# An attention and gMLP block on one core: matrix-engine warm-up matmuls, a last output block in two column halves, and new written-out task orders

## The chip, the cores and the metric

The kernel runs on one core of a Trainium2 chip. The metric is the device time of that core in microseconds (us). The kernel before took 248.39 us (median of 3 runs, 246.49 to 248.95). A core has five engines with a queue of instructions each: PE multiplies matrices (its weight loads have a row of their own, PEld), DVE and ACT work on vectors, POOL does small things, and SP here only issues DMAs. ACT issues a few DMAs too. An engine takes its instructions strictly in the order in which they were written; between engines there are semaphores.

## The reference

The input x is 2048 tokens by 448 features in bf16. Two residual blocks follow each other:

```python
h  = x + A(layernorm(x))          # local attention
h2 = h + B(layernorm(h))          # gMLP
# A: q, k, v = x @ wqkv, 16 heads of 28; token t sees the 8 tokens t, t-2, ..., t-14
#    o = softmax(q k / sqrt(28)) v;  o @ wo
# B: z = gelu(x @ w_in) (1792 columns), z1 = first 896, z2 = layernorm(last 896)
#    g = w_sp @ z2 + b_sp  (2048 x 2048 over the tokens);  (z1 * g) @ w_out
```

## The kernel before

Tokens are held in 16 blocks of 128; block u and block u+8 are worked on together as "unit" u (8 units), on the two halves of the partitions. The work is cut into 667 tasks, each for one engine, with names used here and in the prediction:

- `x0` to `x15`, `xhalo`, `wq`, `wk`, `wv`, `win`, `wsp`: loads (L723, L758, L730, L742, L1124). `wsp` and `tD` are transposing DMAs.
- `bn1`, `rs1`, `nrm1` (L818, L808 or L830, L838): first layer norm of a block: statistics, reciprocal deviation, normalised block. `bnh`, `rsh`, `nrmh`, `tTh`, `evh` do it for the 16 halo rows.
- `tT1_u` with `ev1_u` (L854, L803/L805), or `tD1_u` (L845): unit u transposed by PE and copied out of PSUM, or by a DMA. Units 0 to 2 go the first way.
- `cpq`, `cpk` (L803 on ACT, L805 on DVE): four copies each that spread the loaded q and k weights; the last digit of the name is the column half. `mmq2_0`, `mmk0_2` and so on (L965): q and k projections of a token chunk (first number) for two head groups (or one, in chunk 3); `evq`, `evk` copy them out of PSUM.
- For each attention tile i of nine: `mmv` (L1005, 28 matmuls), `mml` (L1040, 64), `exp` (L1053), `mask` (L1060), `mmr` (L1069), `ln` and `rex`, `mmo` (L1089, 64), `ot` (L1107). Then per unit `mmy` (L1143) and `h` (L1151), and the second layer norm.
- `mmz2` with `ge`, `bn3`, `ag3`, `rs3`, `nrm3` (L1163, L1173, L1179, L1185, L809, L1193): z2 and its layer norm. `mmz1`, `gz1` (L1207, L1217): z1.
- `g` (L1244): the token mixing, 28 groups of 16 matmuls; the first three groups (0_0, 0_1, 0_2) are cut into eight pieces of two, one per unit. `ua`, `um` (L1254, L1262) add the bias and multiply by z1. `wo` (L1273), `oa` (L1281), `st` (L1285): output product, residual and store of each block.

The order of the tasks on every engine is written out: `SEQ` (L41 to L72) holds a list of task numbers per engine, for SP, POOL, DVE, ACT and PE. `Planner.replay` walks the five lists with a model of durations; the model does not change the order, but it picks the PSUM banks and other buffers by the free times it computes. It would also put dummy matmuls (`fill`, L795, on the constant tile `warm`) into predicted idle stretches of PE, provided that the memset of `warm` (`c_warm`) already stands behind it in the walk. In the list of DVE `c_warm` stands among the last tasks, so no dummy matmul is put anywhere. `Sched.issue` turns reads and writes into semaphore waits.

Of the kernel before, what the change touches and what calls it, by code (L numbers as in the profile page):

```python
# [33 lines left out]
PHASES = [(range(0, 9), range(0, 8))]  # L34
WPEN = 200
MPEN = 10.704
OFF = {"q": -124.25, "v": 1265.42, "evv": 569.01, "l": -1263.94, "exp": -259.78, "mask": -1085.83, "r": -1027.56, "o":
       -1264.27, "ln": 1046.18, "ot": 511.44, "y": -65.14, "h": 108.86, "ln2": -195.97, "z2": -1857.43, "ge": 2334.62,
       "n3": 1020.58, "x0": -60.60, "xd": 242.96, "evq": 1087.78, "cp": 975.37, "td": 561.22, "cw": -627.08}
ADJ = ()  # L40
SEQ = (  # L41
# [30 lines left out]
)  # L72
O_AFTER_LN = True
NBANKS = 8
TU = 26.48
NE = 2
NL = 2
NV = 3
SET_E = "natural_log_exp_and_others"
SET_G = "gelu_apprx_tanh_and_others"  # L80

# [152 lines left out]
class Planner:  # L234
# [19 lines left out]
    def pick(self, p, n):  # L254
# [5 lines left out]
        if n == 1:  # L260
            single = sorted((s for s in free if s ^ 1 not in free), key=lambda s: free[s])
            if single:
                return [single[0]]
# [1079 lines left out]
```

## Time and profile before

| | before |
|---|---|
| time, median of 3 runs | 248.39 us (246.49 to 248.95) |
| profiled execution, span | 247.4 us |
| PE busy | 232.1 us, 94% of the span |
| DVE busy | 143.3 us, 58% |
| ACT busy | 91.4 us, 37% |
| POOL busy | 28.8 us, 12% |
| granted clock | 1.00 |

The span runs from the first to the last instruction of the profiled execution, its page gives no other time for it. The span lies inside the three timed runs: 1.0 us under their median and 0.9 us over the fastest. An engine that is not the one everything waits for may idle at no cost; the chain of work that ended last tells which stretches count.

### The profile page before, as it was taken

What the parts mean: (1) busy time and instruction counts of PE and PEld (TensorE: products, weight loads), DVE (VectorE), ACT (ScalarE), POOL (GpSimd) and SP (SyncE); (2) the same over time, 40 slices, a digit from 0 to 9 for tenths busy, and PEclk for the clock granted to TensorE, in tenths of its full rate; (3) what the DMA queues carried; (4) which work ended last, traced back from release to release, by engine and by line L of the source; (5) the groups of instructions that cost most, each with busy time, mean ns of one, the idle gap of its engine ahead of it and who ended that gap; (6) DMA issues with size and microseconds to landing.
All of it is one profiled execution on the core that took longest, in us unless ns stands there. A gap on an engine that the chain in (4) does not pass through costs nothing.

```text
span 247.4 us, 6649 instructions
## 1 busy us (share of the span) xinstructions
PE 232.1 (94%) x3004; PEld 123.7 (50%) x3004; DVE 143.3 (58%) x281; ACT 91.4 (37%) x103; POOL 28.8 (12%) x69
## 2 busy tenths in 40 slices
PE   0399799999999999999999999999999999999995
PEld 0297485445556555555544444444444444444442
DVE  6697847779999897798970022335021407541743
ACT  2668784886979965575740000000000000000000
POOL 2843010000021112104530000000000000000000
DMA  6935965893224976886733333100000000010113
GB/s 159 255 80 61 138 91 98 128 154 71 46 40 85 152 197 124 180 147 150 108 85 85 87 85 85 42 3 0 0 0 0 3 0 0 2 46 29 56 57 111
DMA packets 54436, 20.02 MB, mean 81 GB/s; under 512 B 46584, under 2 KB 54280, under 8 KB 54408
## 3 DMA queue, kind: packets, MB, share of 16 engines
q1 hardware_dynamic: 52584, 18.05, 37.4%
q10 hardware_dynamic: 1824, 1.55, 2.8%
q8 instruction: 23, 0.38, 0.7%
q14 instruction: 5, 0.04, 0.1%
HBM read 6.39 MB, written 1.84 MB: 33 GB/s over the span
## 4 chain that ended last, share of the span: by engine, by line
PE 93%; DMA 3%; issue 1%; ACT 1%; ACTq 1%; DVE 0%
PE psum L1244 39%; PE psum L965 11%; PE psum L1163 9%; PE psum L1273 9%; PE psum L1207 9%; PE psum L1005 5%; PE psum L1143 5%; DMA z2p<-in_A_wqkv_dram 3%; PE psum L1040 3%; PE psum L1089 2%; PE psum L1069 1%; ACT reg L803 1%; ACTq L723 1%; ACT xh L803 0%; ACTq L730 0%
## 5 line engine op out<-in xcount | busy, mean ns | idle before, releaser
L1254 DVE TENSOR_TENSOR ub<-psum,reg 128x512 bf16<-128x512 f32 x28 | 18.8, 687 | 64.3 <-PE psum L1244 64.2
L1244 PE MATMUL psum<-reg,z2p 128*128 128x512 bf16 x224 | 50.0, 379 | 0.0
L1244 PE MATMUL psum<-wspT_lo,z2p 128*128 128x512 bf16 x224 | 49.0, 379 | 0.0
L1244 PEld LDWEIGHTS psum<-wspT_lo,z2p 128*128 128x128 bf16 x224 | 21.8, 98 | 26.6 <-issue 0.4
L1244 PEld LDWEIGHTS psum<-reg,z2p 128*128 128x128 bf16 x224 | 21.9, 98 | 26.1
L965 PE MATMUL psum<-xh,reg 64*128 64x128 bf16 (+3 forms) x448 | 28.5, 290 | 2.8 <-issue 2.0
L965 PEld LDWEIGHTS psum<-xh,reg 64*128 64x128 bf16 x448 | 19.4, 105 | 10.5 <-issue 3.4
L1163 PE MATMUL psum<-w_in,xh 64*128 64x448 bf16 x224 | 22.5, 349 | 0.0
L1273 PE MATMUL psum<-reg 128*128 128x448 bf16 x112 | 22.3, 352 | 0.0
L1207 PE MATMUL psum<-xh,w_in 64*128 64x512 bf16 x196 | 22.2, 376 | 0.0
L818 DVE BATCH_NORM_STATS2 st<-x_tm 128x6 f32<-128x448 bf16 x32 | 19.5, 609 | 1.0 <-DMA x_tm<-in_A_x_dram 0.8
L1179 DVE BATCH_NORM_STATS2 st<-z2p 128x6 f32<-128x448 bf16 x32 | 17.7, 612 | 2.6 <-ACT z2p L1173 2.5
L803 ACT ACTIVATE reg<-psum 128x896 bf16<-128x896 f32 (+3 forms) x21 | 16.8, 824 | 5.8 <-PE psum L965 4.2
L1053 ACT ACTIVATE reg<-psum 128x928 bf16<-128x928 f32 x18 | 16.1, 943 | 6.4 <-PE psum L1040 6.4
L1281 DVE TENSOR_TENSOR tring<-psum,x_tm 128x448 bf16<-128x448 f32 x16 | 9.6, 616 | 14.0 <-PE psum L1273 14.0
L808 POOL TENSOR_SCALAR rs<-mv 128x2 f32<-128x2 f32 x21 | 6.3, 300 | 93.7 <-DVE mv L819 78.4
L1173 ACT ACTIVATE z2p<-psum 128x896 bf16<-128x896 f32 x16 | 14.2, 916 | 6.8 <-PE psum L1163 6.8
L1163 PEld LDWEIGHTS psum<-w_in,xh 64*128 64x128 bf16 x224 | 11.9, 94 | 9.5 <-issue 0.9
L1217 ACT ACTIVATE reg<-psum 128x1024 bf16<-128x1024 f32 x14 | 13.7, 1030 | 7.8 <-PE psum L1207 7.8
L1273 PEld LDWEIGHTS psum<-reg 128*128 128x128 bf16 x112 | 11.0, 98 | 10.6
L1207 PEld LDWEIGHTS psum<-xh,w_in 64*128 64x128 bf16 x196 | 11.1, 94 | 9.7
L809 POOL TENSOR_TENSOR rs<-rs,nhalf 128x2 f32<-128x2 f32 x21 | 15.6, 743 | 1.8
(63 smaller groups left out, 201.2 us busy)
## 6 DMA issues: line engine op xcount, KB each, us to landing
out_dram<-tring SPq DMA_DIRECT2D x16, 112.0 KB, 1.7
x_tm<-in_A_x_dram SPq DMA_DIRECT2D x13, 112.0 KB, 5.7
w_in<-in_B_w_in_dram SPq DMA_DIRECT2D x2, 448.0 KB, 5.5
z2p<-in_A_wqkv_dram ACTq DMA_DIRECT2D x2, 392.0 KB, 6.3
reg<-in_B_w_out_dram SPq DMA_DIRECT2D x1, 784.0 KB, 4.8
w_in<-in_B_w_in_dram SPq DMA_DIRECT2D x2, 336.0 KB, 5.1
reg<-in_B_b_sp_dram SPq DMA_DIRECT2D x1, 512.0 KB, 4.2
reg<-in_A_wo_dram SPq DMA_DIRECT2D x4, 98.0 KB
```

Source lines behind the costliest of these rows:

```text
L803: iss("act", lambda e: e.activation(dst, src, AF.Copy), reads=rd, writes=wr)
L809: iss("pool", lambda e: e.tensor_tensor(dst, dst, nh, ALU.pow), reads=rr + [r_nhalf], writes=rr)
L818: iss("dve", lambda e: e.bn_stats(st[:, b, :], x_tm[:, b, :]), reads=[r_x[b]], writes=[rl[b]])
L965: iss("pe", lambda e, c=c, s=s, gi=gi, lhs=lhs: e.matmul(psum[:, bk[s] * 512 + cw * gi:bk[s] * 512 + cw * gi + cw], lhs, xh[64 * s:64 * s ...
L1053: iss("act", lambda e: e.activation(E[:, es[0], 2 * n:2 * n + 2, :], pair_view(lb, 0, 8 * JW), AF.Exp, scale=SCALE), reads=[r_bank[lb[0]], ...
L1163: iss("pe", lambda e, c=c, s=s: e.matmul(psum[:, zb[s] * 512:zb[s] * 512 + D], xh[64 * s:64 * s + 64, c, HX + 128 * u:HX + 128 * u + 128], ...
L1173: iss("act", lambda e: e.activation(z2p[:, u:u + 9:8, D * k:D * k + D], pair_view(zb, 0, D), AF.Gelu_apprx_tanh), reads=[r_bank[zb[0]], r_ ...
L1179: iss("dve", lambda e, b=b: e.bn_stats(st3[:, b, k, :], z2p[:, b, D * k:D * k + D]), reads=[r_z2[b][k]], writes=[r_st3[b][k]])
L1207: iss("pe", lambda e, c=c, s=s: e.matmul(psum[:, bk[s] * 512:bk[s] * 512 + 512], w_in[64 * s:64 * s + 64, c, 128 * f:128 * f + 128], xh[64 ...
L1244: iss("pe", lambda e, b=b: e.matmul(psum[:, gb[0] * 512:gb[0] * 512 + 512], z2p[:, b, 128 * f:128 * f + 128], src[:, b, 512 * (tc % 2):512 ...
L1254: iss("dve", lambda e: e.tensor_tensor(ub[:, us_[0], :], psum[:, gb[0] * 512:gb[0] * 512 + 512], bb[:, 512 * tc:512 * tc + 512], ALU.add), ...
L1273: iss("pe", lambda e, f=f: e.matmul(psum[:, wb[0] * 512:wb[0] * 512 + D], z1p[f][:, 128 * m:128 * m + 128], w_out[:, f, :], start=(f == 0) ...
```

## The change

1. `c_warm` comes second on DVE instead of near the end. Three new PE tasks hold dummy matmuls of 512 columns on `warm`: `f0` (15, the first task of PE), `f1` (3, after `tT1_0`) and `f2` (3, after `tT1_1`). They write a PSUM bank that nobody reads. The old way of placing fillers is gone.
2. Block 15, the last to be stored, is computed in two halves of 224 columns: its 7 matmuls of 448 columns become 14 of 224, its `oa` and its store become two each. A half has its own PSUM bank and its own slot of the store ring.
3. The constants of the planner's model are different, which can change bank numbers only, and the heuristic scheduler that was unused is deleted.
4. All five lists are new. The heads of the lists, by name (`mml0` and `mmo0` stand for the four tasks of a tile, in the last line `mml3+mml2` for eight that alternate):

```text
SP    before  x0 xhalo x4 x3 x10 x7 x6 x2 x5 x11 wo2 x12 x13 x15 tD1_3 x14 wo3 win1_0 tD1_4 tD1_7 tD1_6 tD1_5
      after   xhalo x0 x4 x3 x5 x11 x13 x7 x2 x10 x12 x6 wo1 x15 tD1_3 x14 win1_0 tD1_5 tD1_7 tD1_6 tD1_4
POOL  before  c_wkp c_wqp c_nhalf c_ident c_eps rs1_1 rsh c_mband c_V c_xpad c_kpad rs1_2
      after   c_V c_eps c_nhalf c_ident c_wkp rsh c_wqp c_kpad c_xpad rs1_3 c_mband c_ones
DVE   before  c_th0 c_wo0 bn1_0 bn1_1 bn1_8 bn1_9 nrm1_0 bnh nrm1_8 nrm1_1 nrm1_9 cpq10 nrmh cpk01 cpk10
              cpq11 evh bn1_2 bn1_10 cpk11 bn1_11 bn1_12 nrm1_2 bn1_3 nrm1_10 bn1_4 cpv10 nrm1_3 nrm1_11
      after   c_th0 c_warm c_wo0 bnh bn1_9 bn1_0 bn1_1 bn1_8 nrm1_1 nrm1_9 nrm1_0 nrmh nrm1_8 cpk11 ev1_0
              cpk00 cpk10 evh cpq01 bn1_11 bn1_3 cpq00 bn1_10 nrm1_3 bn1_2 nrm1_11 cpv10 bn1_13 nrm1_2
ACT   before  x1 x8 x9 wk wq c_tab rs1_0 cpk00 cpq00 ev1_1 ev1_0 evq1_0 wv evk1_0 cpq01 evq0_0 evk1_2 evk0_0
      after   x9 x1 x8 wk wq c_tab rs1_1 rs1_0 cpk01 ev1_1 cpq11 wv cpq10 evk1_2 evk0_0 evk1_0 evq0_2 evq0_0 evk0_2
PE    before  tT1_0 tT1_1 tTh mmq1_0 mmk1_0 mmq0_0 mmk0_0 mmk1_2 mmq0_2 mmk0_2 mmq1_2 tT1_2 mml0 mmv1 mmv0
              mml1 mmv2 mmq2_0 mmr0 mmr1 mmq2_2 mmk2_2 mmk2_0 mmo0 mmv3 mmo1 mml2 mmq3_1
      after   f0 tT1_1 f2 tT1_0 f1 tTh mmk1_2 mmk1_0 mmk0_0 mmk0_2 mmq0_2 mmq0_0 mmq1_2 mmq1_0 mml0 mmv1 mmv0
              tT1_2 mml1 mmr0 mmq2_2 mmk2_2 mmq2_0 mmk2_0 mmo0 mmr1 mmv2 mmv3 mmo1 mml3+mml2 mmq3_2
```

Further on, the last `mmz2` of PE (`mmz2_6_1`) is followed by eight `mmz1` tasks instead of six, and the token mixing starts with `g0_2_0 g0_6_0 g0_1_0 g1_3_0` instead of `g0_2_0 g0_2_1 g0_2_2 g0_1_0 g0_1_1 g0_0_0 g0_0_1 g0_1_2 g0_6_0`. From `g0_4_0` on the order of PE is the same as before up to its end, which is now `wo12_6 wo14_6`, then for block 15 the first six matmuls of either half and the seventh of either half.

The core of the diff, without the lists and the deleted scheduler:

```diff
+        def fill(name, n, deps=()):
+            fb = []
+
+            def em():
+                for _ in range(n):
+                    iss("pe", lambda e: e.matmul(psum[:, fb[0] * 512:fb[0] * 512 + 512], warm[:, 0:128], warm[:, :]),
+                        reads=[r_warm], writes=[r_bank[fb[0]]])
+            return add(name, "pe", 0.216 * n, em, deps=[c_warm] + list(deps), acq=[("ps", 1, fb)], rel=[("ps", fb)], mode="F", nmm=n)
...
+        fill("f0", 15)
+        fill("f1", 3, [pl.named["tT1_0"]])
+        fill("f2", 3, [pl.named["tT1_1"]])
...
+                cols = ((0, D // 2), (D // 2, D)) if m == NB - 1 else ((0, D),)
+                for ci, (d0, d1) in enumerate(cols):
+                    wb, ts_ = [], []
+                    lastw = None
+                    for fs in ((list(range(6)), [6]) if tc == 3 else (list(range(7)),)):
+                        def em(m=m, wb=wb, fs=fs, tc=tc, d0=d0, d1=d1):
+                            for f in fs:
+                                iss("pe", lambda e, f=f: e.matmul(psum[:, wb[0] * 512 + d0:wb[0] * 512 + d1],
+                                                                 z1p[f][:, 128 * m:128 * m + 128], w_out[:, f, d0:d1],
+                                                                 start=(f == 0), stop=(f == FC7 - 1)),
+                                    reads=[r_z1[f][tc], r_wout], writes=[r_bank[wb[0]]])
...
-        pl.run()
+        pl.replay()
```

More of the change, by code (lines that the diff above doesn't have):

```diff
@@ L361, in replay @@
             if e == "pe":
-                if self.filler is not None and self.pools["ps"] and self.filler[0].end is not None:
-                    tf, bank = min(self.pools["ps"])
-                    room = now - max(free["pe"], tf + 0.3, self.filler[0].end + 0.2) - self.FILL[1]
-                    if room > self.FILL[0]:
-                        nf = int(room / self.FILL[2]) + 1
-                        self.fetch(nf, now - room, room, True)
-                        self.filler[1](bank, nf)
                 if t.nmm:
@@ L373, in replay @@
                     pe_mode = t.mode
+                if now - pe_end > (0.6 if warm < self.WARM else 3.0):
+                    warm = 0.0
+                slow = min(dur, (self.WARM - warm) / 2)
+                dur += slow
+                warm += 2 * slow if slow < dur / 2 else self.WARM - warm
+                pe_end = now + dur + extra
             t.start = now
@@ L714, in em @@
                     sch.store_keys.append(key)
[L715 removed]
+            t = add(name, eng, issue, em, deps=deps, rel=rel, nbytes=nbytes)
             t.bw = bw
@@ L1269, in bass_sequential_preLN__sliding_local_dilated__mixer_gmlp__prompt_kernel @@
-                lastw = None
-                for fs in ((list(range(6)), [6]) if tc == 3 else (list(range(7)),)):
-                    def em(m=m, wb=wb, fs=fs, tc=tc):
-                        for f in fs:
-                            iss("pe", lambda e, f=f: e.matmul(psum[:, wb[0] * 512:wb[0] * 512 + D],
-                                                             z1p[f][:, 128 * m:128 * m + 128], w_out[:, f, :],
-                                                             start=(f == 0), stop=(f == FC7 - 1)),
-                                reads=[r_z1[f][tc], r_wout], writes=[r_bank[wb[0]]])
-                    lastw = add("wo%d_%d" % (m, fs[0]), "pe", pe_n(D, len(fs)), em, deps=[t_u[f, tc] for f in fs] + [t_wout, lastw],
-                                prio=P if fs[0] == 0 else P - 20, acq=[("ps", 1, wb)] if fs[0] == 0 else [], mode="F", nmm=len(fs))
@@ new lines, in bass_sequential_preLN__sliding_local_dilated__mixer_gmlp__prompt_kernel, with em @@
+                for ci, (d0, d1) in enumerate(cols):
[8 more added lines that the diff above has]
+                                    reads=[r_z1[f][tc], r_wout], writes=[r_bank[wb[0]]])
+                        first = fs[0] == 0
+                        lastw = add("wo%d_%d_%d" % (m, ci, fs[0]), "pe", pe_n(d1 - d0, len(fs)), em,
+                                    deps=[t_u[f, tc] for f in fs] + [t_wout, lastw],
+                                    acq=[("ps", 1, wb)] if first else [], mode="F", nmm=len(fs))
+                    def em(m=m, wb=wb, ts_=ts_, d0=d0, d1=d1, ):
+                        iss("dve", lambda e: e.tensor_tensor(tring[:, ts_[0], d0:d1], psum[:, wb[0] * 512 + d0:wb[0] * 512 + d1],
+                                                             x_tm[:, m, d0:d1], ALU.add),
+                            reads=[r_bank[wb[0]], r_x[m]], writes=r_tr[ts_[0]])
+                    to_ = add("oa%d_%d" % (m, ci), "dve", dve32(d1 - d0), em, deps=[lastw], acq=[("tr", 1, ts_)], rel=[("ps", wb)])
+                    dma("sp", "st%d_%d" % (m, ci), lambda e, m=m, ts_=ts_, d0=d0, d1=d1: e.dma_start(
+                        OUT[128 * m:128 * m + 128, d0:d1], tring[:, ts_[0], d0:d1]),
+                        128 * (d1 - d0) * 2, deps=[to_], reads=LazyRes(r_tr, ts_), rel=[("tr", ts_)], store=True)
```

402 lines of the change are left out of this document (100 added, 302 removed), and 61 rows, old and new, of the table SEQ.

## The prediction

> **What bounds the kernel now.** I read the page's busy shares and its chain of work that ended last, and then the same chain in order of time, since shares don't tell a stage that runs at half speed from one that runs well.
>
> ```profile
> PE 232.1 (94%) x3004; PEld 123.7 (50%) x3004; DVE 143.3 (58%) x281; ACT 91.4 (37%) x103; POOL 28.8 (12%) x69
> PE 93%; DMA 3%; issue 1%; ACT 1%; ACTq 1%; DVE 0%
> ```
> ```profile
> 2.92 7.07 DMA z2p<-in_A_wqkv_dram
> ...
> 11.52 0.81 ACT xh L803
> ...
> 12.38 9.04 PE psum L965 x164
> 21.41 0.50 PE psum L854 x7
> ...
> 22.56 1.82 PE psum L1005 x34
> 24.38 0.01 issue
> ...
> 26.36 1.45 PE psum L1005 x28
> ...
> 28.68 1.74 issue
> ...
> 117.50 9.07 PE psum L1207 x84
> 126.57 72.63 PE psum L1244 x336
> ...
> 244.59 0.62 DVE tring L1281
> ```
>
> The reader is to see three things. From 12.38 to 244.57 the chain stays on PE, but for one hole of 1.74 us; L1207 runs 84 matmuls in 9.07 us and L1244 336 in 72.63, 216 ns for each full pass of 512 columns, and there is nothing to win in them without less work. Before 12.38 the chain is a load of weights, a copy on ACT and the copy of a transposed unit. And the first projections (L965) take 9.04 us. The windows of that line show at what rate:
>
> ```profile
> 12.38:13.38 1.00, 1.00 (x20) 1.00 (x22) 1.00 0.24 76
> 16.38:17.38 1.00, 1.00 (x24) 1.00 (x22) 1.00 0.88 257
> 17.38:18.38 1.00, 1.00 (x38) 1.00 (x34) 1.00 0.17 35
> 19.38:20.38 1.00, 1.00 (x44) 1.00 (x40) 1.00 0.00 0
> ```
>
> In parentheses stand the matmuls in each us (those on an edge count twice): 20 to 24 up to 17.38, then 38 to 44. The granted clock reads 1.00 in all of them, so it is not in that column that this shows; PE works at about half rate for its first 5.0 us of steady work. All else (tail, 2.8 us from 244.59 to 247.4) is small. So the change can win at the head, in the hole, and in the tail.
>
> **The first projections.** The old list starts with q, whose weights land last:
>
> ```profile
> 7.70 1.51 ACT L803 ACTIVATE reg<-z2p 64x1568 bf16<-64x1568 bf16 x1 [1.70 <-DMA z2p<-in_A_wqkv_dram]
> 10.01 1.51 ACT L803 ACTIVATE reg<-z2p 64x1568 bf16<-64x1568 bf16 x1 [0.80 <-DMA z2p<-in_A_wqkv_dram]
> 14.10 0.60 ACT L803 ACTIVATE reg<-psum 128x512 bf16<-128x512 f32 x1 [0.97 <-PE psum L965]
> 14.57 0.62 DVE L805 COPY reg<-z2p 64x1568 bf16<-64x1568 bf16 x1
> 10.65 0.49 DVE L879 TENSOR_SCALAR thalo<-xhalo,mvh,rsh 16x448 bf16<-16x448 bf16 x1
> 19.89 0.70 DVE L838 TENSOR_SCALAR tring<-x_tm,mv,rs 128x448 bf16<-128x448 bf16 x2
> 3.13 0.63 DVE L818 BATCH_NORM_STATS2 st<-x_tm 128x6 f32<-128x448 bf16 x1 [0.82 <-DMA x_tm<-in_A_x_dram]
> 3.90 0.59 DVE L818 BATCH_NORM_STATS2 st<-x_tm 128x6 f32<-128x448 bf16 x1
> 7.50 1.71 PE L854 MATMUL psum<-ident,tring 128*128 128x128 bf16 x14 [7.50 <-DVE tring L838]
> ```
>
> k is there at 7.7, q at 10.0. The new list starts with `mmk1_2`: it needs `cpk01` (ACT, 7.7 to 9.2) and then `ev1_1` (0.81, to 10.05), and on DVE `cpk11` and `ev1_0`. DVE, as far as its list goes without a wait: the halo's and four block statistics at 0.77 each (3.13 to 3.90) from 3.0 on, when the first loads land, give 6.8; four normalisations at 0.35 and the halo's 0.49, 8.7; `cpk11` 0.62, 9.3, with `tT1_0` meanwhile on PE. `ev1_0` is a copy of 896 bf16 columns out of PSUM, which the trace shows on ACT (0.81) and not on DVE; there twice the addition of 448 f32 columns (616 ns, quoted under the tail) would be 1.2. I take 0.8, the same copy: it ends at 10.1, at most 10.5. So PE starts at about 10.4, **2.0 earlier**. `mmk1_0` then waits for two more DVE copies (to 11.4), 0.2. `mmq0_2` needs `cpq01`, `cpq11` and the banks of `mmk1_2`, which ACT empties behind `cpq11` and `cpq10` (1.5 each) at 13.6; three more groups of k keep PE busy until about then. After that each group of 28 matmuls (0.9) has one ACT copy of 0.6, and DVE's `cpq00`, with `cpq01` and two statistics ahead of it, ends near 14.2: both in time. POOL's memsets change places, all ahead of their first readers.
>
> **The warm-up.** `c_warm` is a memset of 0.5 (its row is quoted under the tail) on DVE ahead of the first statistics, where DVE waits 0.82 for x: free. `f0` can start at 2.0 and runs beside the loads; even at half rate throughout, 15 passes of twice 216 ns end at 8.5, before ACT has finished `cpk01`. `f2` and `f1`, 0.65 each, lie in front of 10.4, where PE has nothing else. No gap before the projections is longer than 1 us. So they run at the later rate: scaling 224 by the window counts, 93 matmuls took the first 5.0 us and 131 the other 4.04; at 31 ns the 93 take 2.8, **2.2 less** (2.5 if exactly half). [...] The trace has 5.0 for this spell, and the sum goes by it.
>
> The projections thus end at 10.4 + 0.2 + 6.9 = 17.5 instead of 21.41: **−3.9**.
>
> **The hole at 28.68.** It falls in the middle of `mmq2_0`, whose data is there: 14 of its 28 matmuls have run. What was late is code. PE's 6,008 recorded instructions pass through 23 packets:
>
> ```profile
> q8 instruction: 23, 0.38, 0.7%
> ```
>
> that is some 260 each, about 130 matmuls with their weight loads. The hole comes behind matmul 478 (14, 7, 224, 7, 64, 56, 64, 28, 14 in PE's order); 128 earlier, behind 350, is the short one at 24.38 (0.01): a block is 128 matmuls. The DMA view, asked in quarters of a us, has one such packet in 17.75 to 18.0, 21.5 to 21.75 and 27.5 to 27.75:
>
> ```profile
> q8 instruction: 1, 0.02, 27.8%
> q8 instruction: 1, 0.02, 35.7%
> q8 instruction: 1, 0.02, 34.6%
> ```
> ```profile
> 14.10 0.60 ACTq L730 DMA_DIRECT2D reg<-in_A_wqkv_dram  x1
> 23.51 0.43 SPq L1114 DMA_DIRECT2D reg<-in_A_wo_dram  x1
> 23.98 0.73 SPq L742 DMA_DIRECT2D w_in<-in_B_w_in_dram  x1
> ```
>
> PE goes on about 2.8 us behind a packet (21.6 to 24.39, 27.6 to 30.42). The shortest spacing is 3.7, and two packets come 3.8 behind the issue of `wv` and 3.6 behind that of `win1_0`: code queues behind the big loads. The new order moves both loads. `wv` is issued beside `cpq11`, at 10.05, so the first packet comes at 13.8 and the second no sooner than 17.5. `win1_0` was issued 3.4 behind the end of the last normalisation for `tD1_3` (20.59), 0.5 of it for `wo3`, which is gone from there. DVE reaches the end of `nrm1_11` at 16.4 (11.4, two copies of 0.62, four statistics of 0.77, two normalisations of 0.35), so `win1_0` is issued at 19.3 and the third packet comes at 22.9.
>
> The three are needed at matmuls 222, 350 and 478 of the new order, which the 21 dummies bring forward: 12 into `mmq1_2`, 20 into `mmv1`, 5 into `mmq2_2`. Unhindered, PE is there at 16.1 (10.6 and 180 at 31 ns), 19.2 and 22.9. The last two are as far behind the projections as matmul 350 and the hole, 2.97 and 7.27, with what now comes later taken off: `tT1_2` 0.50 and 15 matmuls of L1005 at 53 ns from the one, `mmv2` 1.45 and half of `mmq2_0` 0.9 from the other, and 0.5 put on for `mmr0` and five of `mmq2_2`. The code is there at 16.6, 20.3 and 25.7. So the waits add up to 25.7 − 22.9 = 2.8 where before had 1.75: **+1.05**.
>
> **Between 26 and 123.** PE has the same matmuls. The other engines have to come forward by the same 2.85:
>
> ```profile
> 24.00:60.00 36.00, 33.98 (x967) 20.04 (x961) 25.51 (x32) 26.39 (x32) 0.93 (x2) 1.00 0.76 122
> 60.00:126.00 66.00, 65.87 (x1138) 36.47 (x1132) 58.68 (x124) 48.86 (x52) 15.70 (x32) 1.00 0.62 119
> 126.31 2.63 DVE L1193 TENSOR_SCALAR z2p<-z2p,mv,rs 128x896 bf16<-128x896 bf16 x6 [0.90 <-POOL rs L809]
> ```
>
> DVE is idle for 10.5 of 36 us in the first and 7.3 of 66 in the second: it can. One place is tight. `g0_6_0` needs every block of z2, and moves from 16 matmuls (3.45) behind the start of the mixing to two (0.43). DVE's last `nrm3` ended at 128.94, 2.4 behind that start, with 1.1 to spare; now it must end by about 124.1. For its being met: eight `mmz1` (12.1) instead of six (9.07) stand behind the last `mmz2`, so DVE gets its last input 3.0 sooner against the start. I take 0; bounds 0 to +5.
>
> **The tail.** Half an addition is, between `evh` (208 ns for 98 columns) and the whole (616), about 350 ns; two take 700. The first half's last matmul ends only 0.1 before the second's, so DVE ends where it ended, and the store's way out is mostly latency:
>
> ```profile
> out_dram<-tring SPq DMA_DIRECT2D x16, 112.0 KB, 1.7
> L779 DVE MEMSET warm<- 128x512 bf16 x1 | 0.5, 485 | 0.1
> L894 DVE COPY xh<-psum 128x98 bf16<-128x98 bf16 x1 | 0.2, 208 | 0.0
> L1281 DVE TENSOR_TENSOR tring<-psum,x_tm 128x448 bf16<-128x448 f32 x16 | 9.6, 616 | 14.0 <-PE psum L1273 14.0
> ```
>
> 0, within ±0.3. Model constants and the deleted scheduler issue nothing; new bank numbers are in the 0 above.
>
> **The sum.** −3.9 + 1.05 = −2.85 against the execution of 247.4, to 244.55. The page gives that execution no time but its span; the runs lie from 0.9 below it to 1.6 above, and the same difference from their median of 248.39 gives **245.5**. Its own range is 244.6 to 246.8 (`ev1_0` ±0.3, the rate ±0.3, packets ±0.7).
>
> **Rivals.** *Code in time.* If `win1_0` is issued late enough, or the third request soon enough, for the packet to go ahead of it, it comes 3.7 behind the second, at 21.2, and PE waits 1.2; the gain is 4.45; with no wait at all it is 3.9 + 1.75 = 5.65. So 242.7 to 243.9. Against it: both packets that big loads could hold were held. [...] Chance 0.22.
>
> *The hand-over is late.* If `nrm3` stays at 128.94 whatever PE does (DVE is 89% busy from 60 to 126), `g0_6_0` starts at 129.1 instead of 126.57 + 0.43: +2.1 over before, 250.5. It decides from an end of `nrm3` later than 124.1; each us behind that costs one, and the gain is gone at 127. Partial cases are likelier than the whole. Chance 0.20.
>
> *The head doesn't move.* `ev1_0` on DVE or the x loads, now in another order, hold PE to 12, or the dummies don't keep the rate: half of the 3.9 remains while the waits for code stay, 246.5 to 248.4. Chance 0.10.
>
> Forecast 0.42; 0.06 is left for a stall I don't see, slower. About 1% is what a measurement of this kernel can tell from no change, as the three runs spread by 1%; 1% faster is 245.9. Of the forecast 0.26 lies below it, of the third rival 0.02, and the first rival whole: faster 0.50. Slower by 1% (250.9) are 0.06 of the hand-over and the 0.06: 0.12. The rest is 0.38. Range 242.8 to 249.2: it leaves out about 0.05 of the first rival, 0.07 of the hand-over and the unseen stalls.
>
> **What would show it.** In the new trace: dummies from 2 us on; L965 from 10.4 at 38 to 44 per us from its first window; mml0 near 18 to 19; a hole marked issue in `mmq2_2` ending near 25.7 with a code packet 2.8 before it; `nrm3` ending by 124.1 and L1244 without a hole behind its second matmul. A hole at that place, or a long one in the chain at 19 to 26, would make the prediction wrong.

## The result, and the profile after

The changed kernel takes 246.57 us (median of 20 runs, 244.31 to 249.25), the kernel before on the same chip 247.70 (20 runs). The ratio is 0.9939, with a 95% interval of 0.9912 to 0.9967: 0.6% faster, a gain that the interval separates from nothing, but less than the 1% that the prediction asked of "faster" and half of the 1.2% that it forecast. Ratios here leave out executions more than 1.5% longer than the fastest of their kernel, medians are over all of them, so the two can disagree.

| | before | after |
|---|---|---|
| time, median | 247.70 us | 246.57 us |
| profiled execution, span | 247.4 us | 244.4 us (its time: 246.46) |
| first projections, start and end | 12.38, 21.41 us | 10.01, 18.20 us |
| start of the token mixing | 126.57 us | 123.74 us |
| last addition starts | 244.59 us | 241.52 us |

The first fence has the page's busy row of PE and the engine shares of its chain, the second the chain of work that ended last, in order of time (start, duration, what), cut to the stretches that the prediction spoke of. In the changed file L618 is the dummy matmuls, L787 the q and k projections, L825 `mmv`, L859 `mml`, L960 `mmy`, L1060 the mixing, L1099 the residual addition.

```profile
PE 234.2 (96%) x3021; PEld 120.7 (49%) x3032; DVE 142.3 (58%) x283; ACT 88.8 (36%) x104; POOL 26.9 (11%) x67
PE 83%; DMA 9%; DVE 4%; issue 2%; SPq 1%; ACT 0%; DVEq 0%
```
```profile
7.66 0.65 PE psum L618 x3
...
10.07 3.40 PE psum L787 x112
13.47 0.12 issue
13.59 2.08 PE psum L787 x68
15.66 1.13 issue
16.79 1.40 PE psum L787 x44
...
20.01 0.90 issue
...
24.44 6.47 PE psum L787 x112
...
49.45 2.71 DMA reg<-in_A_wo_dram
52.22 1.69 PE psum L960 x8
...
123.58 0.16 issue
123.74 10.74 PE psum L1060 x49
...
241.52 0.06 DVE tring L1099
```

The projections now run at about the full rate from the start, as the windows of L787 show (matmuls per us in the first parentheses; in the first five us before, 20 to 24):

```profile
10.00:11.00 1.00, 0.99 (x32) 1.00 (x34) 1.00 1.10 375
11.00:12.00 1.00, 1.00 (x40) 1.00 (x36) 1.00 1.09 372
12.00:13.00 1.00, 1.00 (x44) 1.00 (x40) 1.00 1.14 260
```

The hole of 1.74 us in the middle of `mmq2_0` is gone. In its place stand 1.13 and 0.90 in the chain, and one more that lies beside it, since from 33 to 52 us the chain follows SP's queue to the weights of the output projection. PE's timeline has that one, ahead of the scores of `mml3` and `mml2`; the second row, from DVE's, is the layer norm on which the mixing waits:

```profile
38.91 0.70 PE L859 MATMUL psum<-reg 32*64 32x58 bf16 x61 [1.21 <-issue]
118.68 3.88 DVE L1010 TENSOR_SCALAR z2p<-z2p,mv,rs 128x896 bf16<-128x896 bf16 x9
```

From one profiled execution to the other the kernel gained 3.0 us; from median to median 1.1. Both need an explanation, and the experiments first had to tell what these holes are.

### The profile page after: what moved, and what is told of

It reads as the page before. It is cut to its first block, busy times and chain, and to the rows that moved or that the text cites. A ratio compares the mean times of both kernels' runs of the same rounds, so it can differ in the third digit from the quotient of the medians.

```text
span 244.4 us, 6704 instructions
## 1 busy us (share of the span) xinstructions
PE 234.2 (96%) x3021; PEld 120.7 (49%) x3032; DVE 142.3 (58%) x283; ACT 88.8 (36%) x104; POOL 26.9 (11%) x67
## 4 chain that ended last, share of the span: by engine, by line
PE 83%; DMA 9%; DVE 4%; issue 2%; SPq 1%; ACT 0%; DVEq 0%
PE psum L1060 39%; PE psum L980 9%; PE psum L1024 9%; PE psum L1089 9%; DMA wspT_lo<-in_B_w_sp_dram 6%; PE psum L787 5%; PE psum L960 4%; PE psum L825 4%; PE psum L859 1%; DMA xh<-tring 1%; PE psum L907 1%; DVE st L639 1%; DMA reg<-in_A_wo_dram 1%; PE psum L675 1%; DVE tring L659 1%
## 5 line engine op out<-in xcount | busy, mean ns | idle before, releaser
L1060 PE MATMUL psum<-reg,z2p 128*128 128x512 bf16 x219 | 49.4, 379 | 0.3
L1060 PE MATMUL psum<-wspT_lo,z2p 128*128 128x512 bf16 x218 | 48.5, 379 | 0.4 <-issue 0.2
L1060 PEld LDWEIGHTS psum<-wspT_lo,z2p 128*128 128x128 bf16 x224 | 21.8, 98 | 26.6 <-issue 0.4
L1060 PEld LDWEIGHTS psum<-reg,z2p 128*128 128x128 bf16 x224 | 21.9, 98 | 26.1
L787 PE MATMUL psum<-xh,reg 64*128 64x128 bf16 (+3 forms) x448 | 26.1, 270 | 1.2 <-issue 1.1
L980 PE MATMUL psum<-w_in,xh 64*128 64x448 bf16 x224 | 22.4, 349 | 0.1
L1089 PE MATMUL psum<-reg 128*128 128x448 bf16 (+1 forms) x119 | 22.3, 341 | 0.0
L787 PEld LDWEIGHTS psum<-xh,reg 64*128 64x128 bf16 x448 | 17.1, 94 | 9.0 <-issue 2.1
L624 ACT ACTIVATE reg<-psum 128x896 bf16<-128x896 f32 (+3 forms) x23 | 19.0, 843 | 3.6 <-PE psum L825 2.5
L1099 DVE TENSOR_TENSOR tring<-psum,x_tm 128x448 bf16<-128x448 f32 (+1 forms) x17 | 9.8, 593 | 14.3 <-PE psum L1089 14.2
L1089 PEld LDWEIGHTS psum<-reg 128*128 128x128 bf16 x119 | 11.6, 98 | 10.2
L980 PEld LDWEIGHTS psum<-w_in,xh 64*128 64x128 bf16 x224 | 10.7, 94 | 10.7 <-issue 0.4
L1024 PEld LDWEIGHTS psum<-xh,w_in 64*128 64x128 bf16 x196 | 9.5, 94 | 11.4 <-ACT reg L1034 0.2
L629 POOL TENSOR_SCALAR rs<-mv 128x2 f32<-128x2 f32 x20 | 5.3, 263 | 87.7 <-DVE mv L640 77.4
```

The lines of the kernel that those rows point to most:

```text
L624: iss("act", lambda e: e.activation(dst, src, AF.Copy), reads=rd, writes=wr)
L787: iss("pe", lambda e, c=c, s=s, gi=gi, lhs=lhs: e.matmul(psum[:, bk[s] * 512 + cw * gi:bk[s] * 512 + cw * gi + cw], lhs, xh[64 * s:64 * s ...
L980: iss("pe", lambda e, c=c, s=s: e.matmul(psum[:, zb[s] * 512:zb[s] * 512 + D], xh[64 * s:64 * s + 64, c, HX + 128 * u:HX + 128 * u + 128], ...
L1024: iss("pe", lambda e, c=c, s=s: e.matmul(psum[:, bk[s] * 512:bk[s] * 512 + 512], w_in[64 * s:64 * s + 64, c, 128 * f:128 * f + 128], xh[64 ...
L1060: iss("pe", lambda e, b=b: e.matmul(psum[:, gb[0] * 512:gb[0] * 512 + 512], z2p[:, b, 128 * f:128 * f + 128], src[:, b, 512 * (tc % 2):512 ...
L1089: iss("pe", lambda e, f=f: e.matmul(psum[:, wb[0] * 512 + d0:wb[0] * 512 + d1], z1p[f][:, 128 * m:128 * m + 128], w_out[:, f, d0:d1], star ...
```

## The experiments

### The kernel before again

No edit.

> The kernel before, unchanged, in a second profile. The changed kernel's profiled execution is 3.0 us shorter in its span than the one of before that the prediction was worked out from, but the medians differ by only 1.1 us and the ratio by 0.6%. Theory A: the execution of before that was profiled was a long one, and the ends of the cold spell and of the holes for code differ from run to run; then this profile's span lies nearer to 246 than to 247.4, and the difference sits before 45 us, in the projections or in the hole at 28.68. Theory B: the head is the same in every execution (projections end at 21.4, hole of 1.7 at 28.7) and the difference lies in what stands around the span. Ratio 1.00 in both.

Measured: ratio 0.9987 (0.9938 to 1.0037), span of the profiled execution 248.8 (time 250.74, the longest of the ten), so theory A's shorter span did not come. Its chain has the holes

```profile
19.94 0.36 issue
24.04 0.47 issue
28.79 1.74 issue
...
59.34 0.69 issue
71.07 0.73 issue
```

The one of 1.74 is the same as before, to a hundredth; the others were not in the first profile of the same kernel, where the row at 24.38 had 0.01. So holes marked issue come and go from execution to execution, and one profile samples them. In 115 further executions of this kernel, taken beside the experiments, the median is 248.12 and the extremes 245.12 and 252.54.

### The new order without the dummies

```diff
-        fill("f0", 15)    -  fill("f1", 3, ...)    -  fill("f2", 3, ...)
+        fill("f0", 0)     +  fill("f1", 0, ...)    +  fill("f2", 0, ...)
```

> The changed kernel without the 21 dummy matmuls (f0, f1, f2 emit nothing), orders unchanged. Warmth decides: PE is at half rate for its first 5 us from 10.0 on, the projections end 2.2 us later and the kernel is 2.2 slower than the changed one (249 us, ratio 1.003). Code decides: the packets come when they come, behind the loads of wv and win1_0, and PE waits less for them the later it arrives; the projections end near 19.4 without the hole of 1.1 at 15.7 instead of at 18.2, the hole of 0.9 in mmv1 is gone too, and by mml1 PE is where the changed kernel was (23.4): 0 to 0.5 slower than the changed kernel (246.6 to 247.1, ratio 0.994 to 0.997).

Measured: 248.03 us, ratio 0.9950 (0.9903 to 0.9996). PE's timeline:

```profile
9.95 9.37 PE L787 MATMUL psum<-xh,reg 64*128 64x142 bf16 x224 [0.53 <-DVE xh L626]
```

The projections take 9.37 us instead of 8.19 with the hole, and no hole stands in them or behind them: the second block's scores start at 23.55, with the dummies at 23.38. Without its hole the changed kernel's would take 7.06, so warm-up saves 2.3 us of streaming, and 2.03 of them went back into two waits for code. The ratio is the one that the theory of code gave. Later this execution has a hole of 2.13 at 79.25, behind 2007 matmuls.

### The old order with the fifteen dummies

The kernel before, with `c_warm` second on DVE and `f0` as PE's first task.

> The old orders with 15 dummy matmuls as PE's first task and the memset of their tile second on DVE; nothing else. Warmth decides: the projections run at 31 ns from 12.4 on and the kernel is 2.2 faster than before (ratio 0.991). Code decides: projections reach matmul 222 at 18.6, and its block comes only behind wv (packet near 17.9, code at 20.7): a hole of 2 us there takes the place of the cold spell, and the later holes come 15 matmuls earlier in the work; 0 to 0.5 faster than before (ratio 0.998 to 1.000), or a little slower.

Measured: 249.04 us, ratio 1.0008 (0.9967 to 1.0050): no gain. The profiled execution (250.89 us) shows two reasons. First a window of all engines over the head (the seventh figure is the granted clock), then PE's and ACT's timelines at 50 us, then the windows there:

```profile
12.00:14.00 2.00, 2.00 (x44) 2.00 (x40) 1.89 (x7) 0.99 (x2) 1.00 (x7) 0.51 0.18 52
...
52.00:54.00 2.00, 1.74 (x12) 0.72 (x14) 0.65 (x1) 2.00 (x4) 0.00 (x0) 0.75 0.81 198
54.00:56.00 2.00, 2.00 (x20) 0.74 (x20) 1.21 (x1) 0.90 (x2) 0.00 (x0) 0.50 1.06 186
56.00:58.00 2.00, 2.00 (x132) 1.25 (x121) 0.92 (x2) 0.31 (x1) 0.00 (x0) 0.90 0.00 0
```
```profile
52.27 2.49 PE L965 MATMUL psum<-xh,reg 64*128 64x512 bf16 x14 [2.11 <-ACT reg L1077]
```
```profile
47.95 2.44 ACT L803 ACTIVATE w_in<-w_in 64x2688 bf16<-64x2688 bf16 x1 [3.04 <-DMA w_in<-in_B_w_in_dram]
```

The fifteen dummies end before 7 us; gaps of 0.6, 1.6 and 0.9 us follow between the transposes, where the changed kernel has `f2` and `f1`, and the clock reads 0.51 as the projections start: the warmth was lost again. And what was won (PE is 3.2 us ahead at 45 us) is lost at 50: ACT stands 3.04 us for `win1_1`, a load that SP's list holds between chained transposes, PE stands 2.11 behind ACT's queue, and then PE runs at half clock. In the last three windows the deficit of the clock is 0.25·2, 0.50·2 and 0.10·2 us, 1.7 together: a spell of 3.4 us at half rate. Its mean clock is 0.986, and five of the other eleven executions have the same within 0.001. The falls are not the whole of it, though: the three executions with a mean clock of 0.999 or more took 247.13, 248.21 and 248.58 us, against a median of 248.57 for the kernel before on that chip, so they do not show a gain of 2.2 either.

### The last block in one piece

```diff
-                cols = ((0, D // 2), (D // 2, D)) if m == NB - 1 else ((0, D),)
+                cols = ((0, D // 2), (D // 2, D)) if m == NB else ((0, D),)
```

> The changed kernel with block 15 in one piece again (7 matmuls of 448 columns, one addition, one store). By the prediction the split is worth 0 within 0.3: the same time as the changed kernel, last addition ending 0.7 after the last matmul in both. If the smaller store counts, 0.2 to 0.3 slower than the changed kernel.

Measured: 246.35 us, ratio 0.9914 (0.9875 to 0.9953), span 244.0. The last addition:

```profile
241.20 0.62 DVE L1099 TENSOR_TENSOR tring<-psum,x_tm 128x448 bf16<-128x448 f32 x1 [0.36 <-PE psum L1089]
```

It ends at 241.82, the two halves ended at 242.2. The split is worth nothing.

### The same streaming in more instructions

```diff
-        fill("f0", 15)                     # 15 matmuls of 512 columns
+        fill("f0", 60, w=128)              # 60 of 128: as many columns, 45 matmuls more
```

> The changed kernel, with the first dummy task as 60 matmuls of 128 columns instead of 15 of 512: the same 7680 columns of streaming, 45 matmuls (90 instructions with their weight loads) more ahead of the first projection. Theory A (the holes stand at fixed counts of instructions, 222 and 350 matmuls): 87 matmuls come ahead of the first projection instead of 42, so the first hole comes after 135 projections of 64 rows instead of 180, at about 13.7 us; the code there cannot move before the x blocks are through at 12.3 to 14.0, so TensorE goes on at 15.1 to 16.8 and stands 1.4 to 3.1 us instead of 1.13; the second hole moves by 45 matmuls as well. Theory B (the hole is a wait for data or for a buffer that the profile does not show): it stays after 180 projections at 15.7. End to end: within 0.5 us of the changed kernel by both.

Measured: 250.19 us, ratio 1.0089 (1.0043 to 1.0134). PE's timeline:

```profile
10.96 4.13 PE L787 MATMUL psum<-xh,reg 64*128 64x142 bf16 x135
15.94 2.67 PE L787 MATMUL psum<-xh,reg 64*128 64x128 bf16 x89 [0.85 <-issue]
...
25.94 0.41 PE L859 MATMUL psum<-reg 32*64 32x58 bf16 x25 [1.79 <-issue]
```

The hole stands behind 135 projections, no longer behind 180, so it goes by the count of instructions, theory A's point exactly. Its size was missed (0.85, since the projections started 0.95 later here), and both theories were wrong about the end: 45 more matmuls with no more streaming cost 3.6 us between the medians. Every later hole falls elsewhere in the order as well, and in the profiles the holes add up to 6.2 us instead of 3.6; beside that, five of the ten executions have a mean clock of 0.993 or less, where the changed kernel has three of twenty. The table gathers the holes marked issue over 0.15 us, in us, by the number of matmuls ahead of them in PE's timeline. Three that fit no step of the others are left out: 0.27 and 0.29 at 820 matmuls in the two profiles of before (where the kernel without dummies waits 0.25 for a transposed x), and 0.16 at 2465, ahead of the mixing, in the one of after:

| matmuls ahead | before | before again | after | no dummies | old order, dummies | sixty short | v weights later |
|---|---|---|---|---|---|---|---|
| 222 | | 0.36 | 1.13 | | | 0.85 | |
| 350 | | 0.47 | 0.90 | | | 1.00 | |
| 478 | 1.74 | 1.74 | | | 0.36 | 1.79 | |
| 858 | | | 1.21 | 0.75 | | 0.44 | 1.38 |
| 1241 | | 0.69 | | | | 1.50 | |
| 1369 | | | | | | 0.19 | |
| 1497 | | | 0.18 | | | | 0.29 |
| 1625 | | 0.73 | | | | | |
| 1753 | | | | | | 0.40 | |
| 1880 | | | | | 0.69 | | |
| 2007 | | | 0.22 | 2.13 | | | |
| sum | 1.7 | 4.0 | 3.6 | 2.9 | 1.1 | 6.2 | 1.7 |

Two orders, with and without dummies, and the places are the same to within two records: steps of 127 to 128 matmuls, that is 256 instructions with the weight loads. Beside them I put, from PE's timeline and the DMA view in narrowing windows, when PE entered a block, when the packet for the next one moved (to within 0.07 us), and when PE entered that one:

| kernel, block entered behind | entered | packet | next block entered | hole |
|---|---|---|---|---|
| after, 94 | 11.62 | 14.03 | 16.79 | 1.13 |
| after, 222 | 16.79 | 18.03 | 20.90 | 0.90 |
| v weights later, 94 | 12.30 | 12.63 | 15.89 | none |
| sixty short, 350 | 20.04 | 23.23 | 25.94 | 1.79 |
| no dummies, 1880 | 75.87 | 78.65 | 81.39 | 2.13 |

In these rows the packet comes after the entry into the block ahead of the one it carries: by 0.3 us where the DMA engines have room (busy share 0.46 from 12 to 13 us with the v weights later), by 1.2 to 3.2 where they are full (1.09 to 1.15 from 11 to 14 us and 1.09 from 17 to 18 in the changed kernel). PE goes on 2.3 to 3.1 us behind the packet at every hole of all the profiles. So, by an estimate from these rows, a block's 128 matmuls must take some 3 to 4 us, more beside big loads, or PE waits; 128 scores take only 1.4 us (64 in 0.7).

### The v weights' load later

```diff
  ACT   ... cpk01 ev1_1 cpq11
- wv cpq10 evk1_2
+ cpq10 evk1_2 wv
  DVE   ... nrm1_11
- cpv10 bn1_13 nrm1_2
+ bn1_13 nrm1_2 cpv10
```

> The changed kernel, with the load of the v weights issued from ScalarE's list three entries later (behind the first of the four 568-column evictions instead of behind the copy of the second q half), and the v weights' copy cpv10 two entries later on VectorE. Readings of the changed kernel: TensorE stands 1.13 us after 222 matmuls (15.66 to 16.79), the code packet it needs moves at 14.03, and until 14.9 the DMA engines are full of x blocks and of the v weights (issued 9.89). Theory A, code queued behind bulk loads: TensorE asks for the next block of 256 instructions when it enters the block before it (after 94 to 96 matmuls, about 11.8), the packet moves as soon as the x blocks are through (12.3 to 13.0), TensorE can go on 2.8 us later (15.1 to 15.8), so the hole at 15.7 shrinks to 0 to 0.3; the second hole (0.90 at 20.0) stays between 0.5 and 0.9, since 128 matmuls of the projections' size take 3.2 us and a packet needs 3.7 to 3.9 from request to use; the second block's scores begin at 22.2 to 22.6 instead of 23.38. Theory B, the fetch has its own pace: packet again at 14.0 and hole again 1.0 to 1.2. End to end both expect little, A -0.3 (the wait of the output projection for its weights at 52.2 grows instead), B 0.

Measured: 245.44 us, ratio 0.9896 (0.9861 to 0.9932).

```profile
10.55 6.78 PE L787 MATMUL psum<-xh,reg 64*128 64x142 bf16 x224
...
37.53 0.71 PE L859 MATMUL psum<-reg 32*64 32x58 bf16 x61 [1.38 <-issue]
```

Theory A held: the load is issued at 11.64 instead of 9.89, the packet moves at 12.63 instead of 14.03, and all 224 projections run without a hole, ending at 17.33 although they start 0.54 later. The second hole went as well (PE waits 0.49 there for the copy of the v weights instead). One profile each would be little, since holes come and go, but others agree: the kernel with the last block whole has the head of the changed kernel, and the same two holes,

```profile
16.92 1.40 PE L787 MATMUL psum<-xh,reg 64*128 64x128 bf16 x44 [1.42 <-issue]
21.06 2.05 PE L825 MATMUL psum<-reg,xh 64*64 64x448 bf16 x37 [1.00 <-issue]
```

and none of the four other kernels below that have the later load and the dummies shows a hole at 222 matmuls. At the end more came of it than either theory gave: 1.1 us between the medians. The ratio lies 0.4% under the changed kernel's; the two intervals still overlap.

### The same without dummies

The two edits together: the v weights later, and no `f0`, `f1`, `f2`.

> The kernel with the v weights' load later, without the three dummy tasks (21 matmuls fewer), so that the worth of the warm-up can be read where the code for the projections comes in time. Theory A (warm-up is worth its cold spell): projections take 9.0 to 9.4 us instead of 6.78, the second block's scores begin at 23.3 to 23.8 instead of 22.05, and of these 1.3 to 1.7 us 0.5 to 1.3 are left at the end: median 246.0 to 246.8. Theory B (code waits in the middle even it out): the hole at 858 matmuls is smaller by about as much as the head is later, and the median is 245.2 to 245.8.

Measured: 249.45 us, ratio 1.0061 (1.0023 to 1.0099). With the later load, then, the 21 dummies are worth 4.0 us between medians, more than the 1.75 that the head shows (scores of the second block at 23.80 against 22.05). Both theories gave less. But the code was not in time here: the projections and the `mmv` behind them wait for it, and the holes add up to 3.6 us in this profile, 1.7 in that of the kernel with dummies:

```profile
18.30 0.85 PE L787 MATMUL psum<-xh,reg 64*128 64x128 bf16 x24 [0.42 <-issue]
22.41 0.95 PE L825 MATMUL psum<-reg,xh 64*64 64x448 bf16 x16 [0.33 <-issue]
```

The profile shows a second cause:

```profile
65.57 4.20 PE L825 MATMUL psum<-reg,xh 64*64 64x448 bf16 x52 [1.49 <-issue]
```
```profile
66.00:68.00 2.00, 2.00 (x28) 1.28 (x24) 1.90 (x4) 0.00 (x0) 0.26 (x1) 0.50 0.83 71
```

A wait for code of 1.49 is followed by a spell of half clock (0.50 in the window); the 52 matmuls take 4.20, where 56 take 2.85 in the profile of the kernel with dummies. Seven of the twelve executions have a mean clock of 0.993 or less, three of twelve with the dummies. So the 4.0 is what this pair of kernels shows, not the price of the cold spell at the start.

### The output weights ahead of the transposes, too

```diff
  SP    ... tD1_7 tD1_6 tD1_4
- wsp0_0 wo2 wsp0_8 win1_1 wsp0_1 wo3 wsp0_9 wo0 win0_0
+ wo2 wo3 wo0 win1_1 wsp0_0 wsp0_8 wsp0_1 wsp0_9 win0_0
```

with the later v weights.

> The same edit, and the three late loads of the output projection's weights and the second load of w_in's first half go on SyncE ahead of the first of the chained w_sp transposes (about 21 us) instead of between them. Theory A (code behind bulk loads, and the head's gain stopped at 52.2 us by the weights queued behind the transposes): the first output projection begins 0.5 to 1.3 us before the 52.2 of the changed kernel, without a wait for a DMA, and the median is 0.5 to 1.0 us below the changed kernel's 246.6 (ratio to the kernel before 0.988 to 0.992). Theory B (the head is given back to code waits later, wherever the order leaves a dense stretch of small matmuls): the projection begins earlier, but holes by issue of 0.5 to 2 us between 37 and 82 us take it back, and the ratio stays 0.993 to 0.997. If the transposes, now about 4 us later, become what the mixing waits for, its start is later than 123.7 with a DMA as the releaser.

Measured: 245.21 us, ratio 0.9897 (0.9849 to 0.9946). `mmy0` starts at 50.76 without its wait, as A said, but the result is that of the kernel with the v weights later alone, and holes of 0.90 at 858 and 0.82 at 1497 stand where B had them. The loads' place is worth nothing measurable.

### The old order with dummies and earlier loads

To the old order with the fifteen dummies: `win1_1`, `wo0` and `wo1` on SP ahead of the first of the chained transposes.

> The kernel before with the 15 dummy matmuls first (as in the run of the old order above), and on SyncE the second load of w_in's first half and the two late loads of the output weights ahead of the chained w_sp transposes instead of between them. Theory A (in the old order the head's 3.2 us were lost at 50 us: ScalarE stood for this load, TensorE stood 2.11 us behind it and then ran at half clock for about 2 us): the load lands before 40 us, ScalarE's copy of it does not wait, no hole at 50, clock 1.00 from 50 to 56, and the time falls to 245.0 to 247.0 (ratio 0.985 to 0.994). Theory B (the order of the middle can't use an earlier head): another wait of 1 to 3 us takes its place before the mixing starts and the ratio stays above 0.996.

Measured: 251.04 us, ratio 1.0132 (1.0079 to 1.0186), slower. ACT's copy no longer waits and PE has no hole at 50, but

```profile
40.62 0.60 PE L965 MATMUL psum<-xh,reg 64*128 64x512 bf16 x3 [0.88 <-issue]
...
57.49 0.21 PE L1089 MATMUL psum<-reg 64*32 64x58 bf16 x4 [2.34 <-issue]
```

stand at 860 and 1243 matmuls, and a half-clock spell of 3.4 us behind the second (the clock reads 0.90, 0.50 and 0.75 in the windows of two us from 56 to 62). Theory B, with code as the wait that takes over: PE entered the block at 1118 late in the last `mmv` at 53.8 by its count, the packet came at 54.72, and the next 124 matmuls, small ones, took 1.4 us.

### Wide projections ahead of the small scores

```diff
  PE    ... mmo1
- mml3_00 mml2_00 mml2_01 mml3_01 mmq3_2 mml2_10 mml2_11 mml3_10 mml3_11 mmq3_3
+ mmq3_2 mmq3_3 mml3_00 mml2_00 mml2_01 mml3_01 mml2_10 mml2_11 mml3_10 mml3_11
```

with ACT's `evq3_2 evq3_3` ahead of `exp3_0`, and the later v weights.

> The kernel with the v weights' load later, and of the third chunk's q projections the two tasks mmq3_2 and mmq3_3 (28 matmuls of 512 columns) ahead of the scores of the second and third token blocks instead of between and behind them (their two evictions on ScalarE ahead of exp3_0 likewise). Theory A (a block of 128 matmuls can't be used until 3.4 to 3.9 us after the block ahead of it was entered): matmuls 733 to 858 now take 2.8 us and TensorE stands 1.38 us at 858; with 28 wide ones among them instead of 17 the same stretch takes over 4 us and that hole is gone or under 0.3. The projections may stand up to 0.6 for the transposed x, which lands at about 34.1. All four score tasks are through 0.7 to 1.1 us earlier for the same work (by 38.8 to 39.3 with mmq3_3 behind them; the work of both stretches ended at 39.9). End to end -0.5 to -1.0 against 245.4 if the wait for the output projection's weights at 50.9 does not take it, about 0 if it does. Theory B (the hole belongs to the scores' operands, not to the count): a hole of 1 us or more stays ahead of the scores wherever they stand.

Measured: 245.57 us, ratio 0.9941 (0.9901 to 0.9982). The hole at 858 is gone, as A had it, and the wait for the transposed x is 0.29. The gain is given back at once, in PE's timeline, to engines that now get the scores later:

```profile
38.87 1.47 PE L787 MATMUL psum<-xh,reg 64*128 64x512 bf16 x12 [0.45 <-ACT reg L871]
...
46.97 3.20 PE L787 MATMUL psum<-xh,reg 64*128 64x512 bf16 x28 [0.74 <-DVE reg L626]
```

### Everything together

The last edit, the loads on SP, the copy `cpv10` one entry earlier, and the last block whole.

> The same, and with it: the output projection's weights and w_in's second load ahead of the chained transposes on SyncE, the v weights' copy one entry earlier on VectorE (it made TensorE wait 0.49 at 18.3), and the last output block in one piece as in the kernel before. Theory A: the sum of the holes removed (1.0 at 858, 0.5 at 18.3, 0.24 at 50.9), 0.8 to 1.7 us under the 245.3 of the two kernels with the v weights later: 243.6 to 244.5, ratio to the kernel before 0.983 to 0.987. Theory B (TensorE enters each block from 56 to 75 us 2.3 to 2.9 us after its packet, and packets come 3.4 to 3.7 apart, so an earlier start there only makes those waits longer): 245.0 and more, ratio 0.988 to 0.990, with holes by issue at 1242, 1497, 1753 or 2007 matmuls that add up to what was gained.

Measured: 247.71 us, ratio 1.0000 (0.9960 to 1.0040), though the profiled execution has a span of 243.8 (time 246.34). The ratio is neither theory's, and none of B's holes is there; five of the twelve executions have a mean clock of 0.993 or less. A hole of 1.35 stands at 476 matmuls, which no theory had put there; the next run has it too.

### The v weights later, their copy earlier

The kernel with the later v weights, with `cpv10` between `bn1_13` and `nrm1_2`.

> The kernel with the v weights' load later, its copy cpv10 one entry earlier on VectorE (behind bn1_13, one entry behind its place in the changed kernel), to have the worth of the later load a second time, with the 0.49 us that TensorE waited for the copy taken out. Theory A (the code packet ahead of the v weights is worth the 1.13 us hole): no hole at 222 matmuls, TensorE no longer waits for the copy, and either the 0.49 is gained or a code wait of 0.1 to 0.4 stands at 350 matmuls in its place; median 244.6 to 245.6, ratio 0.987 to 0.993. Theory B (the 245.4 of the run with the later load was the scatter of the executions): 246.2 to 246.9, as the changed kernel.

Measured: ratio 0.9891 (0.9832 to 0.9949), profiled execution 244.49 us with a span of 242.7, the shortest of the study; yet in 8 of its 12 executions the mean clock is 0.993 or less, and these take 247.3 to 252.1, so that the median is 248.79. The ratio, which rests on five executions here, agrees with the worth of the later load; it does not confirm it, as over all executions this kernel is no faster than the one before (248.79 against 248.14). The wait of 0.49 became one for code of 0.51 at 350 matmuls (A's alternative), and

```profile
24.40 6.17 PE L787 MATMUL psum<-xh,reg 64*128 64x256 bf16 x109 [1.35 <-issue]
```

is the collision that the prediction feared for the changed kernel: PE entered the block behind 350 matmuls at 19.19, `win1_0` had been issued at 18.14, its data filled the DMA engines until 21.9, and the packet moved at 21.77, 3.6 behind that issue. With the later copy `win1_0` went out 0.73 later (18.87), PE entered 0.39 later (19.58), and the packet moved at 20.19, ahead of the same data. This says why a small step on DVE moved a hole; it does not say why the clock fell so often, since the profiled execution is one without a fall.

## Why the prediction was right or wrong

**The number.** 245.5 was predicted and 246.57 measured, in the range and in the forecast's own one. Profile against profile, the sum said −2.85 and the spans say −3.0. It is nearer than its terms were, and that is luck, as the terms below show.

**The first projections, right.** PE starts them at 10.01 (10.4 predicted; `ev1_0` takes 0.62 on DVE where I took 0.8, the 0.2 between the first groups is not there).

**The warm-up, right in size.** 180 matmuls in 5.66 us are 31.4 ns each, I took 31. Without their hole the projections would have ended at 17.07: −4.34 instead of −3.9. The 5.0 us of the cold spell were those of one execution (the last section has others). That PE keeps its rate over gaps of up to 1 us was my estimate: the longest gap between the first dummy and the projections is 0.32 here and the rate held, while in the old order, with gaps of 0.6, 1.6 and 0.9, it was lost.

**Waits for code, right in mechanism, one of three missed.** PE goes on at 16.79 and 20.90 (16.6 and 20.3 predicted), at the matmuls named. The third wait, to 25.7, did not come: DVE reached the end of `nrm1_11` at 15.6, 0.8 sooner than I had it, SP needed 2.0 us behind it where I took 2.9, so `win1_0` went out at 17.63 instead of 19.3. Its data filled the DMA engines until about 21.2, the packet moved at 22.4, and PE reached that block at 24.9 and went on without a hole. 2.03 of holes instead of 2.8: the term is +0.28, not +1.05.

**Between 26 and 123, wrong.** "PE has the same matmuls" and therefore 0 was the step that failed. By the two terms above PE should have been 4.06 ahead; the mixing starts 2.83 earlier. The 1.2 between lie in what I had counted as unchanged: a new hole of 1.21 at 858 matmuls and smaller ones of 0.18 and 0.22 at 1497 and 2007, in place of 0.36 that the kernel before lost there (0.27 at 39.91, 0.09 at 70.21). I had found the rule (a packet for 128 matmuls, 2.8 us before PE goes on) and applied it only to the first 26 us. Two errors, −0.4 and −0.8, and one of +1.2 cancelled, by chance.

**The hand-over, right.** The last `nrm3` ends at 122.56, 1.2 ahead of the mixing; its rival is refuted. The third rival is, too: the head moved fully. The first had one thing right, that the third wait would not come, but for another reason: `win1_0` went ahead of the packet, and early enough.

**The tail, right:** the split is worth nothing by the run with the block whole. A half of 56 KB lands 1.6 us behind its issue, a whole store of 112 KB 1.7.

**From the profile to the median, wrong.** The page of before gave no time; I set its span of 247.4 under the 248.39 of three runs. In the study a span lies about 2.0 under its time (1.8 to 2.5 in the profiled executions), so this execution took about 249.4, an estimate, 1.7 over its kernel's median of 247.70, while the changed kernel's profiled one is 0.1 under its own. The three runs' median was high by 0.7 as well. What makes an ordinary execution of before 1.7 shorter than the profiled one isn't shown; the hole at 478 has that size, but both profiles that I have of that kernel contain it.

**What the parts are worth.** Fifteen dummies alone in the old order, their warmth lost again: nothing (1.0008). The new order alone: 0.9950, both: 0.9939 here and 0.9914 with the last block whole. So of the change as made, the dummies' share can't be told from zero, and the prediction's 2.2 us for them was paid back in code. With the v weights' load later they go with 4.0, waits for code and mid-kernel falls of the clock included; what warmth alone is worth at the end stays open.

## What to carry to other kernels

Count matmuls per code block, as one counts bytes: in the table of packets PE stood still behind four blocks of 128 that took 3.2 to 4.1 us and not behind one of 3.59, so 3.5, more beside big loads, is my estimate of what a block has to take, and the warm-up here gave 2.03 of its 2.3 us back in such waits; look for the boundary in multiples of 128 (here from 94 on) and put wide matmuls, or a big load's issue, on the right side of it. Then look at the end of the kernel too: the wide matmuls here removed a hole and gained nothing. A change of list order moves every later boundary against the work and every load against the packets, so price those over the whole dense stretch, not where the edit stands. And take the spread of executions before believing a profile: the same kernel had 1.7 and 4.0 us of such holes in two profiles.

## What was not expected of the hardware

- A code packet behind a big load stopped PE: with the issue of a 392 KB load 1.75 us later (11.64 instead of 9.89) the packet moved at 12.63 instead of 14.03, and a hole of 1.13 was gone.
- 45 short matmuls with the streaming of none cost 3.6 us between medians, 2.8 between the profiled spans.
- Half-clock spells in mid-kernel last 3.4 us by the granted clock in all three profiles that show one behind a hole (2.11, 2.34 and 1.49 us long), and cost 1.7 each. Holes of 2.13 (no dummies), 1.79 (sixty short) and 1.74 (before again) were followed by no fall, so the length of the hole does not decide.
- Clock is lost in nearly equal steps. In the executions of the twelve runs a mean clock under 0.998 is 0.991 to 0.993, 0.985 to 0.986 or 0.98, with none between: 1.7 to 2.2, 3.5 to 3.7 or 5.0 to 5.1 us lost of the span, as by one, two or three spells of 3.4 us at half rate. The old order with dummies has such a spell in its head, too (0.51 and 0.64 in the windows from 12 to 16 us). In the changed kernel's profile the clock falls only at 243.77, behind the last matmul. What decides whether a hole is followed by a spell was not shown.
- The first cold spell does not appear in the clock column: it reads 1.00 over 20 to 24 matmuls per us before the change and over 32 to 44 after it. The records begin only with the first change to full clock (at 4.83 us in the changed kernel, where the dummies' weight loads go from one in 0.43 us to one in 0.2; at 15.80 without its dummies, where the windows of two us have 36, 41 and 46 matmuls up to 16 us and 80 in the next), and the column reads 1.00 where there is none. The first profile of the kernel before has no record at all, so the 1.00 given for it is no reading. From the start of the projections to that first record it is 5.9 us without the dummies, 4.1 without them and with the later load, 3.9 in the second profile of before, so the length of the spell differs between executions.
